# Layer 1's keys and queries by seven block products of a pair of row tiles, in place of row tile by row tile

## The chip, the cores and the metric

The kernel runs on one core of a Trainium2 chip. The metric is the device time of one execution in microseconds; less is better. Before the change it is 1144.76 us, the median of three runs (1144.38 to 1146.51).

## The reference, cut to what matters

Two layers, each a linear attention block and a gated MLP on x of 2048 rows by 512 columns, with residuals. Both layers use the same weights.

```python
def _A_ref(x, wqkv, wo):                 # H = 32 heads of 16 columns
    q, k, v = split(x @ wqkv)            # 512 -> 3 x 512
    phi = lambda t: jnp.where(t > 0, t + 1, jnp.exp(t)) + 1e-6
    pq, pk = phi(q), phi(k)
    kv = jnp.einsum("bhsd,bhse->bhde", pk, v)
    z = jnp.einsum("bhsd->bhd", pk)
    num = jnp.einsum("bhqd,bhde->bhqe", pq, kv)
    den = jnp.einsum("bhqd,bhd->bhq", pq, z)[..., None] + 1e-6
    return (num / den) @ wo
def _B_ref(x, w1, w3, w2):               # 512 -> 1792 -> 512
    return (silu(x @ w1) * (x @ w3)) @ w2
x = x + _A_ref(_layernorm(x), wqkv, wo);  x = x + _B_ref(_layernorm(x), w1, w3, w2)
x = x + _A_ref(_layernorm(x), wqkv, wo);  x = x + _B_ref(_layernorm(x), w1, w3, w2)
```

## The kernel before, in words

**Numbers in two parts.** Every operand of TensorE is a sum of two float16 numbers, a high and a low part. `mm` multiplies in three passes (high by high, low by high, high by low), so one product of 128 contracted rows is three matmuls.

**One layer.** `attention` goes over the 16 row tiles of 128 rows. For a tile, ACT normalises the row (`keys_rows`, `normalise`), its parts are made, and one DMA transpose of 8 blocks of 128 x 128 turns both parts (`keys_turn`); the turned rows are kept in HBM (`xt_d`) for the queries. The key product of a tile is 4 blocks of 128 features x 3 passes = 12 matmuls of 512 columns into one PSUM bank (`pk`). ACT reads the bank twice (L1257, L1258), takes an exponential, DVE joins them (L1268), and the result is split into parts again (L1316, L1325). `gram` multiplies the parts of keys by the parts of the rows, 12 matmuls of 512 columns a tile, into four banks (`gt0` to `gt3`) that add up over all rows. Then the Gram is scaled and split (L1362 to L1366), multiplied by the value weights (`kv`), masked, and multiplied by the output weights (`pm`), which gives a matrix `m_s`. The queries follow tile by tile: 12 matmuls (`pq`), phi, weighing (`weigh_in`, `weigh_out`), a transpose, 12 matmuls by `m_s` (`po`), and an add into the rows (`attn_add`). Layer 1's queries load their turned rows again from `xt_d`.

**The MLP** goes over passes of 512 rows and groups of hidden columns. It already uses a scheme of seven block products in place of eight (`P1` to `P7` in `mlp_group`): the rows are taken as quarters of two pairs of row tiles by two halves of features, the weights as quarters too, and sums of quarters are multiplied. Each of its products is of 256 columns; three of the seven banks' sums share a bank (`ba`, `bb`, `bc`), from which ACT copies and DVE adds between products. In layer 0's MLP a generator `background` prepares weights in the gaps (`HOOKS` says how many steps it takes after each group).

**The order.** The instructions of each engine stand in an order that is written out by hand: `ORDER` numbers the instructions of each engine as they were recorded and lists the numbers in the order in which they shall run; `arrange` adds that as dependences. An engine runs its list from first to last, so an instruction that waits holds all behind it.

## Time and profile before

| | |
|---|---|
| median of three runs | 1144.76 us |
| profiled execution | 1145.35 us, of which 1143.3 us span |
| granted clock of TensorE | 1.000 |
| busy share of the span | PE 99%, weight loads 75%, DVE 71%, ACT 56%, POOL 35% |
| DMA | 146.91 MB, mean 128 GB/s |
| layer 1's keys | from about 571 to 664 us |
| layer 1's queries | from about 664 to 753 us |

The span is the time from the first to the last instruction on the chip; the execution has about 2 us around it. PE is TensorE's matmuls and PEld its weight loads, DVE is VectorE, ACT is ScalarE, POOL is GpSimd, SP issues all the DMAs here. Nearly all matmuls stand on line 904, in `mm`, so the profile's rows are told apart by the bank that they write.

### The profile page before, as it was taken

How to read it: one execution, taken by the hardware profiler on the slowest of the kernel's cores; microseconds unless marked ns; L12 is line 12 of the kernel's file. 1: busy time of each engine (PE TensorE's matmuls, PEld its weight loads, DVE VectorE, ACT ScalarE, POOL GpSimd, SP SyncE). 2: the span in 40 equal slices, each digit the busy share in tenths (PEclk: the TensorE clock that was granted, in tenths of full speed). 3: DMA queues.
4: the chain of work that ended last, by engine and by line, in shares of the span. 5: the costliest groups of instructions: out<-in, count | busy, mean ns of one | idle time of the engine just before them, and what ended most of it. 6: DMA issues, size and time to landing. Idle time of an engine off the chain costs nothing.

```text
span 1143.3 us, 21778 instructions
## 1 busy us (share of the span) xinstructions
PE 1132.4 (99%) x8820; PEld 859.4 (75%) x8820; DVE 816.8 (71%) x1422; ACT 635.7 (56%) x1081; POOL 395.7 (35%) x494
## 2 busy tenths in 40 slices
PE   8999999999999999999999999999999999999998
PEld 3445445888888888888854454478888888888887
DVE  6888888897888888778773376748856566556556
ACT  6677878765545444334466644676544344353442
POOL 6641697411100304113674215761152120213113
PEclk9999999999999999999999999999999999999999
DMA  9996865796572221111343515955052350202001
GB/s 274 299 262 226 234 128 103 216 264 189 188 255 102 84 84 65 65 66 66 84 120 96 171 44 111 181 142 138 11 146 77 125 235 1 84 20 93 15 20 56
DMA packets 162549, 146.91 MB, mean 128 GB/s; under 512 B 129552, under 2 KB 138000, under 8 KB 157840
## 3 DMA queue, kind: packets, MB, share of 16 engines
q1 hardware_dynamic: 162448, 145.52, 43.5%
q8 instruction: 69, 1.13, 0.4%
q14 instruction: 32, 0.26, 0.1%
HBM read 72.35 MB, written 41.68 MB: 100 GB/s over the span
## 4 chain that ended last, share of the span: by engine, by line
PE 95%; DMA 2%; DVE 2%; POOL 0%; SPq 0%; issue 0%; ACT 0%; DVEq 0%; ACTq 0%; POOLq 0%
PE bb L904 25%; PE po L1740 20%; PE bc L904 13%; PE pq L904 7%; PE gt L904 7%; PE po L904 7%; PE ba L904 6%; PE pk L904 6%; PE po L1760 3%; DMA arena<-in_A_x_dram 1%; DMA arena<-arena 0%; PE kv L904 0%; PE pm L904 0%; DVE arena L828 0%; DVE st L866 0%
## 5 line engine op out<-in xcount | busy, mean ns | idle before, releaser
L904 PEld LDWEIGHTS <-arena 128*128 128x128 f16 x6360 | 618.0, 98 | 243.0 <-issue 4.6
L904 PE MATMUL bb<-arena 128*128 128x256 f16 x2688 | 349.0, 273 | 0.0
L1740 PE MATMUL po<-arena 128*128 128x256 f16 x2058 | 289.3, 273 | 0.0
L1695 ACT ACTIVATE arena<-bb 128x512 f32<-128x512 f32 x196 | 115.8, 594 | 209.8 <-PE bb L904 163.9
L1740 PEld LDWEIGHTS <-arena 128*128 128x128 f16 x2058 | 201.0, 98 | 24.4 <-ACT arena L1654 0.2
L904 PE MATMUL bc<-arena 128*128 128x256 f16 x1344 | 180.6, 273 | 1.4 <-DVE arena L1596 1.4
L1698 DVE TENSOR_TENSOR arena<-arena,bc 128x512 f32<-128x512 f32 x112 | 76.6, 684 | 87.4 <-ACT arena L1695 50.4
L1789 DVE SCALAR_TENSOR_TENSOR arena<-po,scalars,arena 128x256 f32<-128x256 f32 (+1 forms) x180 | 101.5, 585 | 34.6 <-PE po L1740 19.0
L1650 ACT ACTIVATE arena<-arena,scalars 128x512 f32<-128x512 f32 (+1 forms) x112 | 74.5, 666 | 85.9 <-DVE arena L1698 74.0
L1656 DVE TENSOR_TENSOR arena<-arena 128x1280 f16<-128x1280 f32 (+1 forms) x90 | 104.7, 1170 | 23.4 <-ACT arena L1654 23.3
L1654 ACT ACTIVATE arena<-arena 128x512 f16<-128x512 f32 (+1 forms) x112 | 100.9, 904 | 34.2 <-DVE arena L1669 15.7
L1651 DVE SCALAR_TENSOR_TENSOR arena<-arena,scalars 128x512 f32<-128x512 f32 (+1 forms) x112 | 79.2, 709 | 48.0 <-ACT arena L1650 46.5
L904 PE MATMUL ba<-arena 128*128 128x256 f16 x672 | 92.6, 273 | 0.0
L904 PE MATMUL pk<-arena 128*128 128x512 f16 x384 | 88.1, 379 | 2.9 <-DMA arena<-arena 1.8
L1656 POOL TENSOR_TENSOR arena<-arena 128x512 f16<-128x512 f32 x22 | 27.7, 1261 | 176.1 <-ACT arena L1654 133.1
L904 PE MATMUL gt<-arena 128*128 128x512 f16 x384 | 87.1, 379 | 0.2 <-POOL arena L1284 0.2
L904 PE MATMUL po<-arena 128*128 128x512 f16 x384 | 86.5, 379 | 0.0
L904 PE MATMUL pq<-arena 128*128 128x512 f16 x384 | 86.5, 379 | 0.0
L1797 POOL TENSOR_TENSOR arena<-arena 128x512 f32<-128x512 f32 x27 | 37.2, 1378 | 115.1 <-DVE arena L1789 115.1
L881 ACT ACTIVATE arena<-arena,nb_all,rs_all 128x512 f32<-128x512 f32 x64 | 51.0, 805 | 8.5 <-POOL nb_all L878 6.5
L1666 POOL TENSOR_TENSOR arena<-arena 128x256 f32<-128x256 f32 x10 | 7.6, 765 | 131.2 <-DVE arena L1651 131.2
L1581 POOL TENSOR_TENSOR arena<-arena 128x512 f16<-128x512 f32 x32 | 38.0, 1188 | 33.6 <-ACT arena L816 32.8
(163 smaller groups left out, 1279.6 us busy)
## 6 DMA issues: line engine op xcount, KB each, us to landing
arena<-xb_d SPq DMA_DIRECT2D x12, 1792.0 KB, 7.8
xb_d<-arena SPq DMA_DIRECT2D x8, 1792.0 KB, 7.3
xt_d<-arena SPq DMA_DIRECT2D x32, 256.0 KB, 2.6
arena<-xt_d SPq DMA_DIRECT2D x32, 256.0 KB, 3.2
arena<-in_B_w_dram SPq DMA_DIRECT2D x8, 896.0 KB, 5.8
arena<-in_B_w_dram SPq DMA_DIRECT2D x28, 256.0 KB, 3.6
w_d<-arena SPq DMA_DIRECT2D x4, 1792.0 KB, 8.1
arena<-w_d SPq DMA_DIRECT2D x4, 1792.0 KB, 8.2
```

The source lines that it names most:

```text
L881: nc.scalar.activation(dst, x_sb[:, t, :], AF.Identity, scale=rs_all[:, t : t + 1], bias=nb_all[:, t : t + 1],)
L904: nc.tensor.matmul(dst, lhs(a, k), rhs(b, k), start=first and k == 0 and i == 0, stop=last and k == n - 1 and i == len(PASSES) - 1, skip_g ...
L1581: low.tensor_tensor(nat[:, 1, :], to, nat[:, 0, :], OP.subtract)
L1650: nc.scalar.activation(t, gate, AF.Silu, scale=info["u1"])
L1651: nc.vector.scalar_tensor_tensor(t, up, info["hid"], t, OP.mult, OP.mult)
L1654: nc.scalar.activation(hs[:, 0, lo:hi], t[:, lo:hi], AF.Copy)
L1656: engine.tensor_tensor(hs[:, 1, lo:hi], t[:, lo:hi], hs[:, 0, lo:hi], OP.subtract)
L1695: nc.scalar.activation(dst, bank_, AF.Copy)
L1698: nc.vector.tensor_tensor(dst, dst, bank_, OP.add)
L1740: nc.tensor.matmul(po[:, i * HALF : (i + 1) * HALF], hs[:, a, qx, cs], w2[:, b, qw, :], start=g == ends[0] and i + a + b == 0, stop=g == e ...
L1789: nc.vector.scalar_tensor_tensor(dst, src, cb, to, OP.mult, OP.add)
L1797: engine.tensor_tensor(x0, x0, u[:, 0::2], OP.add)
```

## The change

In layer 1, `attention7` takes the place of `attention`. It goes over eight pairs of row tiles. A pair of tiles by two halves of features gives four quarters; four sums of quarters are made (DVE, L1573 to L1576), and all seven are turned by two DMA transposes, one of 12 blocks (the quarters that the Gram needs too) and one of 16 (the four sums). The weights of keys and queries are prepared in the same way in layer 0's last MLP passes (`att7`: seven parts of two halves each), the queries' stored in HBM (`q7_d`) and loaded in layer 1. A pair is then multiplied by `products7`: seven products of 6 matmuls of 256 columns, where three banks `kb`, `ka`, `kc` (`qb`, `qa`, `qc` for queries) take their sums, ACT takes out four of the results and DVE adds three. Later steps on keys and queries work on a pair at once (1024 columns). The Gram, the output product and the MLPs have the same matmuls as before.

```diff
+    def att7(name, i):
+        raw = view(AT_RAW, F32, NK, D)
+        nc.sync.dma_start(raw, wqkv_r[:, i])
+        ...
+        def part(n, src):
+            split_late(wk7[:, 0, :, n, :], wk7[:, 1, :, n, :], src, scale)
+        a11, a21, a12, a22 = quads
+        for n, src in ((0, a11), (1, a12), (2, a22)):
+            part(n, src)
+        for to, a, b, op in ((a22, a21, a22, OP.add), (a21, a11, a21, OP.subtract),
+                             (a11, a22, a11, OP.subtract), (a12, a12, a11, OP.subtract)):
+            nc.gpsimd.tensor_tensor(to, a, b, op)
+        for n, src in enumerate(quads):
+            part(3 + n, src)
...
+    def pair_turn(p, xts, nats):
+        b11, b21, b12, b22 = (q7[:, i, :] for i in range(4))
+        t = view(rows_at[1], F32, 4, HALF)
+        nc.vector.tensor_tensor(t[:, 0, :], b12, b11, OP.subtract)
+        nc.vector.tensor_tensor(t[:, 1, :], b22, t[:, 0, :], OP.subtract)
+        nc.vector.tensor_tensor(t[:, 2, :], b22, b12, OP.subtract)
+        nc.vector.tensor_tensor(t[:, 3, :], b21, t[:, 1, :], OP.subtract)
+        ...
+        xt = xts[p] = xt7_ring.next(F16, 28, P)          # two slots
+        nc.scalar.activation(hi0, q7[:, 0:2, :], AF.Copy)
+        nc.gpsimd.tensor_copy(hi1, q7[:, 2:4, :])
+        nc.gpsimd.tensor_tensor(lo0, q7[:, 0:2, :], hi0, OP.subtract)
+        nc.gpsimd.tensor_tensor(lo1, q7[:, 2:4, :], hi1, OP.subtract)
+        nc.sync.dma_start_transpose(xt[:, :12, :], nb[:, D:])
+        nc.scalar.activation(nt[:, 0], t, AF.Copy)
+        nc.gpsimd.tensor_tensor(nt[:, 1], t, nt[:, 0], OP.subtract)
+        nc.sync.dma_start_transpose(xt[:, 12:, :], nt.rearrange("p a q n -> p (a q n)"))
+        nc.sync.dma_start(xt7_d[:, p], xt)
...
+        product(bb, P1, True, False)          # 2 blocks of features x 3 passes, 256 columns
+        take(0, 0, bb)                        # ACT
+        product(bc, P5, True, False)
+        take(1, 1, bc)
+        product(bb, P6, False, False)
+        take(1, 0, bb)
+        product(bc, P3, False, True)
+        add(1, 0, bc)                         # DVE
+        product(bb, P7, False, False)
+        add(1, 1, bb)
+        product(ba, P2, True, True)
+        add(0, 0, ba)
+        between()
+        product(bb, P4, False, True)
+        take(0, 1, bb)
...
+        def query7(p):
+            ...
+            products7(xqs.pop(p), wq7, banks, *taken(r, info["u7q"], ones[:, 0:1]))
+            nc.scalar.activation(e, r, AF.Exp, bias=minus_one)
+            nc.vector.scalar_tensor_tensor(r, e, 1.0, r, OP.min, OP.max)
+            if p + 2 < NP:
+                load7(p + 2)                  # 896 KB
+        def weigh_out7(p):
+            ...
+                engine = nc.vector if p in (0, 2, 4, 6) else nc.gpsimd
...
-        attention(layer, ready, prep, before_gram)
+        (attention7 if layer else attention)(layer, ready, prep, before_gram)
...
 ORDER = {
     "PE": (
-        "0-56 69-80 57-68 93-104 84-89 117-128 81-83 90-92 105-107 111-116 141-152 108-110 "
...
```

`ORDER` is written anew for all engines and the whole program. `HOOKS` gives `background` 28 more steps after four groups in layer 0 (`0:0` becomes `7:0`), and group 3 of the MLP weights is fetched again at the start of layer 1's MLP, because its slot holds the new key weights.

The following rows show what stands in a row on an engine before and after, for the three places of which the prediction speaks. Repeated rows, and TensorE's weight loads, are left out.

TensorE, the middle of layer 1's keys, before: `pk` with its number is one tile's bank, each row 12 matmuls; `gt0` to `gt3` are the Gram's banks, each row 3 or 6 matmuls.

```order
L904 MATMUL pk_7194<-arena_66 128x512
L904 MATMUL pk_7240<-arena_66 128x512
L904 MATMUL gt2_6835<-arena_66 128x512
L904 MATMUL pk_7286<-arena_66 128x512
L904 MATMUL gt1_6834<-arena_66 128x512
L904 MATMUL gt0_6833<-arena_66 128x512
L904 MATMUL gt3_6836<-arena_66 128x512
```

The same place after, one pair from P1 to P4: P1 is the first row, then 3 matmuls each into two Gram banks, then P6, P5, P2, P7, P3 of 6 matmuls each, 3 Gram matmuls, P4, and the Gram's others.

```order
L945 MATMUL kb_7245<-arena_66 128x256
L945 MATMUL gt0_6954<-arena_66 128x512
L945 MATMUL gt1_6955<-arena_66 128x512
L945 MATMUL kb_7245<-arena_66 128x256
L945 MATMUL kc_7247<-arena_66 128x256
L945 MATMUL ka_7246<-arena_66 128x256
L945 MATMUL kb_7245<-arena_66 128x256
L945 MATMUL kc_7247<-arena_66 128x256
L945 MATMUL gt3_6957<-arena_66 128x512
L945 MATMUL kb_7245<-arena_66 128x256
L945 MATMUL gt2_6956<-arena_66 128x512
```

The tile by tile products have become narrow ones that come back to the same bank `kb` four times and to `kc` twice, with Gram matmuls between them.

ACT, the same stage, before: L1257 and L1258 read the bank, L1259 is the exponential, L816 a row's high part, L1316 a key's high part.

```order
L1257 ACTIVATE arena_66<-pk_7055,scalars_81 128x512
L1259 ACTIVATE arena_66<-arena_66 128x512
L1257 ACTIVATE arena_66<-pk_7102,scalars_81 128x512
L1258 ACTIVATE arena_66<-pk_7102,scalars_81 128x512
L1259 ACTIVATE arena_66<-arena_66 128x512
L816 ACTIVATE arena_66<-arena_66 128x512
L1258 ACTIVATE arena_66<-pk_7055,scalars_81 128x512
L1316 ACTIVATE arena_66<-arena_66,scalars_81 128x512 x2
```

After, for the pair whose products are shown above: L1632 takes a result out of a bank (here of P1, P6, P5 and P4, in this order), L1678 is the high part of the pair before, L1589 that of the four row sums of a later pair, L922 normalises, L1673 and L1674 are the Relu and the exponential.

```order
L1632 ACTIVATE arena_66<-kb_7245,scalars_81 128x256
L1678 ACTIVATE arena_66<-arena_66,scalars_81 128x1024
L1632 ACTIVATE arena_66<-kb_7245,scalars_81 128x256
L1589 ACTIVATE arena_66<-arena_66 128x1024
L1632 ACTIVATE arena_66<-kc_7247,scalars_81 128x256
L922 ACTIVATE arena_66<-arena_66,nb_all_91,rs_all_90 128x512 x2
L1632 ACTIVATE arena_66<-kb_7245,scalars_81 128x256
L1673 ACTIVATE arena_66<-arena_66,scalars_81 128x1024
L1674 ACTIVATE arena_66<-arena_66 128x1024
```

Between two takes that TensorE's next product needs there now stands an instruction of 1024 columns.

DVE, between the keys and the queries of layer 1, before: L1362 scales a Gram bank, L1366 makes a low part, L1270 to L1569 are the first steps on query tile 0.

```order
L1362 TENSOR_TENSOR arena_66<-gt1_6834,arena_66 128x512
L1362 TENSOR_TENSOR arena_66<-gt3_6836,arena_66 128x512
L1366 TENSOR_TENSOR arena_66<-arena_66 128x512 x2
L1362 TENSOR_TENSOR arena_66<-gt2_6835,arena_66 128x512
L1362 TENSOR_TENSOR arena_66<-gt0_6833,arena_66 128x512
L1366 TENSOR_TENSOR arena_66<-arena_66 128x512
L1270 SCALAR_TENSOR_TENSOR arena_66<-arena_66 128x512
L1552 SCALAR_TENSOR_TENSOR arena_66<-arena_66 128x512
```

After: L1716, L1730, L1733, L1747, L1748 and L1751 are the steps on query pair 0 (the first two, one and two instructions, stand ahead of the rows shown); L1776 scales a Gram bank, L1778 makes a low part, L1636 adds a product of query pair 1.

```order
L1733 TENSOR_REDUCE arena_66<-arena_66 128x32
L1747 TENSOR_SCALAR arena_66<-arena_66 128x32
L1776 TENSOR_TENSOR arena_66<-gt0_6954,arena_66 128x512
L1776 TENSOR_TENSOR arena_66<-gt2_6956,arena_66 128x512
L1748 RECIPROCAL arena_66<-arena_66 128x32 x2
L1751 TENSOR_TENSOR arena_66<-arena_66 128x512
L1776 TENSOR_TENSOR arena_66<-gt1_6955,arena_66 128x512
L1778 TENSOR_TENSOR arena_66<-arena_66 128x512
L1636 SCALAR_TENSOR_TENSOR arena_66<-qb_7720,scalars_81,arena_66 128x256
L1636 SCALAR_TENSOR_TENSOR arena_66<-qc_7722,scalars_81,arena_66 128x256
L1776 TENSOR_TENSOR arena_66<-gt3_6957,arena_66 128x512
L1778 TENSOR_TENSOR arena_66<-arena_66 128x512 x2
```

Steps on the queries, which stood behind the Gram's four banks, now stand ahead of and between them.

300 lines of the change are left out of this document (278 added, 22 removed), and 763 rows, old and new, of the table ORDER.

## The prediction

> **What bounds the kernel now.** I read the page first: which engine is never idle, at what clock, and which engine the chain that ended last runs through.
>
> ```profile
> PE 1132.4 (99%) x8820; PEld 859.4 (75%) x8820; DVE 816.8 (71%) x1422; ACT 635.7 (56%) x1081; POOL 395.7 (35%) x494
> PEclk9999999999999999999999999999999999999999
> PE 95%; DMA 2%; DVE 2%; POOL 0%; SPq 0%; issue 0%; ACT 0%; DVEq 0%; ACTq 0%; POOLq 0%
> ```
>
> A busy share of 99% does not prove much by itself, since the ends of matmuls are modelled. So I asked next what TensorE waited for over the whole run (its three longest rows: total us, times, longest) and what its timeline looks like in the stage that changes, layer 1's keys.
>
> ```profile
> PE pk L904 <- DMA arena<-arena: 1.8, 3, 0.8
> PE pm_k L765 <- DVE scalars L762: 1.6, 1, 1.6
> PE bc L904 <- DVE arena L1596: 1.4, 1, 1.4
> ```
>
> ```profile
> 605.41 2.75 PE L904 MATMUL pk<-arena 128*128 128x512 f16 x12
> 608.00 2.75 PE L904 MATMUL gt<-arena 128*128 128x512 f16 x12
> 610.59 5.34 PE L904 MATMUL pk<-arena 128*128 128x512 f16 x24
> 615.77 2.75 PE L904 MATMUL gt<-arena 128*128 128x512 f16 x12
> ```
>
> The reader should see the starts: 605.41, 608.00, 610.59, 615.77 are 2.59, 2.59 and 5.18 us apart, so 12 matmuls always take 2.59 us and no gap lies between key and Gram matmuls. The waits are single events of under 2 us. TensorE's queue is the kernel, and a matmul taken out of it is time taken out, as long as no other engine becomes late.
>
> The second question is what a matmul costs at the two widths. These are rows of the chain of waits, in order of time, the first from layer 1's keys, the second from the MLP, which already multiplies by seven block products of 256 columns:
>
> ```profile
> 648.96 5.18 PE pk L904 x24
> 766.13 3.93 PE bb L904 x36
> ```
>
> A 512-column matmul takes 5.18/24 = 0.2158 us, a 256-column one 3.93/36 = 0.1092 us. Half the width costs half the time (51%), although each has its own weight load.
>
> **What comes out of TensorE's queue.** Before, two row tiles of keys are 2 x 12 matmuls of 512 columns: 24 x 0.2158 = 5.18 us. After, a pair is 7 products x 2 blocks of 128 features x 3 passes = 42 matmuls of 256 columns: 42 x 0.1092 = 4.59 us. That is 0.594 us less for each pair; 8 pairs, keys and queries, make 16 x 0.594 = **9.5 us** less. Gram, output and MLP matmuls keep number and width. Nothing hides this gain and nothing is needed to release it: the queue has no gaps there. The most it can give is 1145.35 - 9.5 = 1135.85 for the profiled execution.
>
> The Trainium skill speaks against this: "TensorE: Matmul & The Clock Gate", section "Back-to-back issue gap", gives a stream of weight loads and matmuls about 81 ns a matmul at 128 columns and 131 ns at 512, so that halving the width saves much less than half. By it a pair would be an estimated 3.1 us before and 3.4 to 5.5 us after, a loss. This trace disagrees: 109 ns and 216 ns.
>
> **What the change adds beside TensorE.** The stages by windows (us; PE, PEld, DVE, ACT and POOL busy): two windows that hold about the last four of layer 0's twelve MLP passes, then layer 1's keys, then its queries. The five columns before the clock are the engines' busy time.
>
> ```profile
> 457.00:515.00 58.00, 58.00 (x534) 51.99 (x532) 43.02 (x72) 22.53 (x37) 10.30 (x9) 1.00 0.17 65
> 515.00:571.00 56.00, 56.00 (x515) 50.06 (x514) 44.11 (x82) 26.03 (x43) 25.54 (x29) 1.00 0.25 76
> 571.00:664.00 93.00, 93.00 (x476) 46.52 (x474) 45.23 (x74) 57.90 (x91) 42.58 (x83) 1.00 0.43 119
> 664.00:753.00 89.00, 89.00 (x463) 43.15 (x461) 65.37 (x132) 55.42 (x114) 48.39 (x54) 1.00 0.57 122
> ```
>
> The prices come from groups of instructions by shape (busy us, mean ns of one):
>
> ```profile
> L1257 ACT ACTIVATE arena<-pk,scalars 128x512 f32<-128x512 f32 x32 | 21.7, 681 | 36.9 <-PE pk L904 36.8
> L1258 ACT ACTIVATE arena<-pk,scalars 128x512 f32<-128x512 f32 x32 | 24.4, 767 | 0.0
> L1791 ACT ACTIVATE arena<-po,scalars 128x256 f32<-128x256 f32 x36 | 16.9, 469 | 30.4 <-PE po L1740 23.2 <-DVE arena L1797 4.6 <-POOL arena L1667 2.5
> L1631 ACT ACTIVATE arena<-arena 128x1024 f16<-128x1024 f32 x16 | 16.8, 1048 | 5.9 <-DVE arena L1627 3.8 <-POOL arena L1627 2.1
> L1789 DVE SCALAR_TENSOR_TENSOR arena<-po,scalars,arena 128x256 f32<-128x256 f32 x108 | 50.0, 478 | 17.3 <-ACT arena L1791 8.4 <-POOL arena L1798 6.0 <-PE po L1740 2.0
> L1667 DVE TENSOR_TENSOR arena<-arena 128x256 f32<-128x256 f32 x39 | 18.8, 482 | 0.3
> L1637 POOL TENSOR_TENSOR arena<-arena 128x1024 f16<-128x1024 f32 x9 | 19.8, 2205 | 2.1 <-ACT arena L1631 2.1
> ```
>
> *Keys, 93.0 - 4.75 = 88.2 us to do it in.* DVE: each pair gains three adds from PSUM (L1789's kind, 0.478) and four row sums (L1667's kind, 0.482), 3.36 us; 45.2 + 8 x 3.36 = 72.1 us, 82%. ACT: two passes over PSUM for each tile, 16 x (0.681 + 0.767) = 23.2 us, become four copies of a quarter and one pass of 1024 for each pair, 8 x (4 x 0.469 + 1.05) = 23.4 us; the high part of the four row sums adds 8 x 1.05 = 8.4; 57.9 + 8.6 = 66.5 us, 75%. POOL: the low part of the sums adds 8 x 2.2 = 17.6 to 42.6: 60.2 us, 68%. All fit, none by so much that order in the queue would be indifferent.
>
> *Order in ACT's queue.* What can hold TensorE is the shared bank: the next product into `kb` waits until ACT has copied the last one out, and P3 waits for the copy of P5 out of `kc`. From the end of P1 of a middle pair, P3 is due after two Gram groups (6 x 0.2158 = 1.29) and P6, P5, P2, P7 (4 x 0.655): 3.91 us. On ACT the copy after P6 starts at 1.95, then stands a 1024 pass (1.05) ahead of P5's copy: 1.95 + 0.47 + 1.05 + 0.47 = 3.94 and the hand-over. So P3 comes on time or about 0.2 us late, 0 to 1.4 us over the six pairs that look like this. Two rows of ACT's timeline say which end is nearer:
>
> ```profile
> 667.43 0.67 ACT L1261 ACTIVATE arena<-pq,scalars 128x512 f32<-128x512 f32 x1
> 668.00 0.68 ACT L1262 ACTIVATE arena<-pq,scalars 128x512 f32<-128x512 f32 x1
> ```
>
> Instructions of 0.68 us start 0.57 us apart, so sums of durations are upper bounds. I take 0.5 us.
>
> *Between keys and queries.* `kv` waits for all of the Gram's scaled parts. In the new order TensorE has 24 wide and 72 narrow matmuls between the last product of query pair 0 and `kv`: 24 x 0.2158 + 72 x 0.1092 = 13.0 us. DVE meanwhile must do the weighing of pair 0 and the Gram's parts, which the old order put mostly after:
>
> ```profile
> L1362 DVE TENSOR_TENSOR arena<-gt,arena 128x512 f32<-128x512 f32 x8 | 5.1, 682 | 0.1
> L1570 DVE RECIPROCAL den<-den 128x32 f32<-128x32 f32 x32 | 11.1, 348 | 2.3 <-ACT den L1556 1.9
> L1569 DVE TENSOR_SCALAR den<-den 128x32 f32<-128x32 f32 x20 | 7.8, 388 | 0.3
> L828 DVE SCALAR_TENSOR_TENSOR arena<-arena,scalars 128x1024 f16<-128x1024 f32 x8 | 10.1, 1277 | 0.0
> ```
>
> It starts after the product, its copy and the exponential, 0.66 + 0.47 + 1.05 = 2.2 us; then one of 1.28, thirteen of about 0.68, two each of 0.35 and 0.39 and two adds of 0.48: 12.5, so 14.7 against 13.0. That is up to 1.7 us late, and about 0.7 with starts 0.08 us closer than durations; I take 0.8. `pm` then has 18 narrow matmuls (1.97 us) as cover for a DVE, an ACT and a DVE step of some 0.65 each: 0 to 0.6 late, I take 0.3.
>
> *Queries, 89.0 - 4.75 = 84.3 us.* DVE gains 24 adds of 0.478, 11.5 us, and of its ten row normalisations, the two rows below, it keeps eight: 65.4 + 11.5 - 1.4 = 75.5 us, 90%. This is the tightest place.
>
> ```profile
> L1573 DVE TENSOR_TENSOR arena<-pq,den 128x512 f32<-128x512 f32 x7 | 4.8, 687 | 0.2
> L1573 DVE TENSOR_TENSOR arena<-arena,den 128x512 f32<-128x512 f32 x3 | 2.1, 685 | 0.0
> ```
>
> TensorE's order there puts output matmuls between P7 and P4, so I take 0.4 us, with 0 and 1.9 (half an add, 0.24, for each of eight pairs) as bounds.
>
> *Transposes and stores.* A pair is turned by one transfer of 12 and one of 16 blocks instead of two of 8, and stored and loaded in 896 KB instead of 2 x 256 KB. The nearest rows are the MLP's transposes of 14 blocks and the weights' transfers of 896 KB (us to landing):
>
> ```profile
> DMA to landing us min/median/max: 3.9/4.1/6.3
> w_d<-arena SPq DMA_DIRECT2D x3, 896.0 KB, 9.6
> arena<-w_d SPq DMA_DIRECT2D x3, 896.0 KB, 6.4
> ```
>
> A slot of the two for turned rows is free after P4 of pair p and wanted by P1 of pair p + 2, 42 wide and 42 narrow matmuls later: 13.6 us. Both transposes one behind the other need 8.2; with a store ahead of them 6.4 + 8.2 = 14.6, but P5, the first to read the second transfer, begins 0.655 + 1.29 + 0.655 = 2.6 us after P1, so 16.2 us are there. I cost it at nothing; the cover is those 13.6 us, and the bound is 0 to 1 us for each of six pairs.
>
> *Layer 0's last passes* gain the seven parts of both weights: 14 high parts on ACT, 14 low parts on DVE, 8 sums on POOL.
>
> ```profile
> L826 ACT ACTIVATE arena<-arena,scalars 128x512 f16<-128x512 f32 x38 | 26.3, 713 | 1.9 <-PE bb L904 0.9 <-DVE scalars L778 0.6 <-DMA arena<-in_B_w_dram 0.3
> L828 DVE SCALAR_TENSOR_TENSOR arena<-arena,scalars 128x512 f16<-128x512 f32 x38 | 29.1, 783 | 0.9 <-ACT arena L826 0.9
> L954 POOL TENSOR_TENSOR arena<-arena 128x512 f32<-128x512 f32 x4 | 5.1, 1269 | 14.7 <-DMA arena<-in_B_w_dram 14.0 <-DVE arena L828 0.6
> ```
>
> That is 10.0 us of ACT, 11.0 of DVE, 10.2 of POOL in 114 us, where DVE stands at 87.1: 98.1 us, 86%, and TensorE has no wait. Nothing on the path; bound 0 to 5.5 if half of DVE's part came in front of MLP steps.
>
> **The sum.** 1145.35 - 9.5 + 0.5 + 0.8 + 0.3 + 0.4 = 1137.85 for an execution like the profiled one, which stands 0.6 above the median of the runs (1144.76). So 1137.3.
>
> **The rivals.** (a) *The order holds:* waits from none to all bounds at once, 1.4 + 1.7 + 0.6 + 1.9 = 5.6 us: 1135.3 to 1140.9. For it: TensorE's short list of waits, though the MLP shares its banks in the same way. Chance 0.70. (b) *Evictions eat most of it:* copies and adds come late by 0.35 to 0.55 us for each of 16 pairs, 5.6 to 8.8 us: 1140.9 to 1144.1. For it, DVE at 90% in the queries; 0.12, of which 0.05 within 0.2% of no change. (c) *DVE becomes the bound of the queries, slower:* the add after P7 stands behind the three 1024-wide steps of the pair before (3 x 1.28 = 3.8 us) and P4 behind it; with three products as cover (1.96) some 1.9 us remain, 8 x 1.9 = 15 us, less 9.5: 1150. It decides from 9.5/8 = 1.2 us a pair (1.5 to be measured as slower). Against it: the output matmuls placed there, 2.59 us a tile. 0.09. (d) *Turned rows late* by 1.2 us for six pairs, 7 us: 1142.3; 0.03, half of it no change. (e) *Weight loads do not hide under narrow matmuls*, so that the saving isn't there: 18 more loads a pair at 98 ns are 1.76 us, less 0.594, 16 times:
>
> ```profile
> L904 PEld LDWEIGHTS <-arena 128*128 128x128 f16 x6360 | 618.0, 98 | 243.0 <-issue 4.6
> ```
>
> +18.7 us, 1163; the MLP's 0.1092 us speaks against it, 0.02. By the section named above it would be this one. (f) *Layer 0's added work shows:* 5.5 us, 1142.8 at worst; 0.04, of which 0.015 no change.
>
> **The numbers.** The likeliest is (a), 1137.3. The range goes from 1134.4, 0.9 below (a)'s lower end (half of the 1.8 us that TensorE waits for the opening's transposes, whose order is new too), to 1142.5, which takes in (a), half of (b), and parts of (d) and (f): about 0.8. 0.2% is 2.3 us, about what a measurement here can tell from no change. Faster: 0.70 + 0.07 + 0.015 of (d) + 0.025 of (f) = 0.81; same: 0.05 + 0.015 + 0.015 = 0.08; slower 0.09 + 0.02 = 0.11.
>
> **What would show it.** Right: narrow key and query matmuls 0.109 us apart; keys and queries together about 7.5 us shorter; TensorE's waits for `kb`, `kc`, `qb` on ACT or DVE under 3 us in all; one visible wait ahead of `kv`. Wrong: TensorE waiting for DVE's adds in the queries by more than 1 us a pair, for a transpose ahead of P1 or P5, or new waits in layer 0.

## The result, and the profile after

The changed kernel takes 1146.41 us (median of 22 runs, 1144.44 to 1153.02), the kernel before 1144.53 in the same comparison (22 runs): 1.0018 times as long, with a 95% interval of 1.0009 to 1.0026. It is slower by about 0.2%, where 0.65% faster was forecast, and lies outside the range of 1134.4 to 1142.5 us.

The page of the changed kernel's profile: busy time, granted clock, and the shares of the chain that ended last.

```profile
PE 1126.6 (98%) x9108; PEld 887.6 (78%) x9108; DVE 853.8 (75%) x1468; ACT 656.7 (57%) x1099; POOL 422.4 (37%) x477
...
PEclk9999999999999999999999999999999999999999
...
PE 86%; DVE 5%; ACT 3%; POOL 2%; DMA 2%; issue 1%; SPq 0%; DVEq 0%; POOLq 0%; ACTq 0%
```

TensorE is busy 5.8 us less than before, at the same clock, but the chain leaves it: 86% where it was 95%. What it waited for, longest first (total us, times, longest):

```profile
PE bc L945 <- DVE arena L2053: 1.9, 1, 1.9
PE po L945 <- DMA arena<-arena: 1.9, 1, 1.9
PE qc L945 <- ACT arena L1632: 1.2, 1, 1.2
...
PE gt L945 <- POOL arena L1652: 1.0, 1, 1.0
...
PE kc L945 <- DMA arena<-arena: 0.8, 1, 0.8
PE po L2095 <- DVE arena L2144: 0.7, 1, 0.7
PE qb L945 <- DVE arena L1636: 0.6, 1, 0.6
...
PE qa L945 <- DVE arena L1818: 0.6, 1, 0.6
```

There is no one culprit: every row shown is a single event, and DVE, ACT, POOL and the transposes are all among the releasers. The windows again, layer 0's last passes, then the keys and the queries at their new places (the last one ends some microseconds before the queries' last output matmuls):

```profile
457.00:515.00 58.00, 57.33 (x526) 51.15 (x524) 49.01 (x80) 30.04 (x49) 21.52 (x17) 1.00 0.38 130
515.00:571.00 56.00, 56.00 (x515) 50.20 (x513) 49.38 (x92) 31.18 (x49) 28.95 (x32) 1.00 0.26 74
571.00:660.00 89.00, 86.84 (x634) 61.55 (x632) 58.86 (x106) 65.30 (x88) 56.21 (x66) 1.00 0.77 202
660.00:745.00 85.00, 80.21 (x554) 52.09 (x553) 71.50 (x115) 52.01 (x92) 41.42 (x31) 1.00 0.57 129
```

Before, TensorE was busy for the whole of all four windows. Now 2.2 us are missing in the keys and 4.8 in the queries, though no other engine is full: DVE stands at 71.5 of 85 us there (84%), POOL at 41.4.

To see where time went I split the distance from TensorE's first matmul to its last in two: what its matmuls take one behind the other (0.216 us for 512 columns, 0.109 for 256; for the few other shapes the median distance of their starts), and the *gaps*, by which two starts lie further apart than that. Before: 1129.0 + 9.2 us. After: 1119.5 + 19.9. The matmuls are shorter by 9.5 us, as worked out (their distances are 0.109 and 0.216 us in both traces), and the gaps are longer by 10.7. The table gives the gaps of every kernel by stage (us from the span's start), worked out in the same way from the starts in each trace.

| kernel | opening, to 60 | layer 0, 60 to 300 | 300 to 571 | keys, 571 to 660 | queries, 660 to 720 | tail, from 720 | all | time, us | ratio to before (interval) |
|---|---|---|---|---|---|---|---|---|---|
| before | 7.6 | 1.7 | 0.0 | 0.0 | -0.1 | -0.1 | 9.2 | 1144.53 | 1 |
| after | 6.4 | 3.6 | 0.8 | 3.4 | 3.8 | 2.0 | 19.9 | 1146.41 | 1.0018 (1.0009 to 1.0026) |
| e1 | 7.4 | 2.3 | 0.8 | 2.0 | 3.8 | 2.0 | 18.2 | 1144.81 | 0.9998 (0.9989 to 1.0007) |
| e2 | 9.4 | 2.5 | 0.8 | 3.4 | 2.8 | 0.2 | 19.0 | 1143.96 | 0.9989 (0.9980 to 0.9997) |
| e3 | 8.1 | 3.9 | 0.8 | 3.4 | 0.9 | 1.2 | 18.3 | 1142.16 | 0.9977 (0.9969 to 0.9986) |
| e4 | 7.8 | 4.6 | 1.7 | 3.4 | 3.5 | 2.0 | 23.0 | 1149.89 | 1.0045 (1.0032 to 1.0057) |
| e5 | 9.2 | 4.7 | 0.2 | 6.1 | 5.5 | 9.2 | 34.8 | 1159.28 | 1.0127 (1.0114 to 1.0140) |
| e6 | 7.9 | 2.4 | 0.8 | 2.8 | 3.8 | 2.0 | 19.6 | 1146.32 | 1.0013 (1.0004 to 1.0022) |
| e7 | 6.3 | 3.7 | 0.8 | 1.4 | 0.0 | -0.1 | 12.0 | 1138.27 | 0.9940 (0.9927 to 0.9953) |
| e8 | 5.9 | 2.4 | 0.2 | 3.6 | 4.0 | 3.9 | 20.0 | 1147.29 | 1.0027 (1.0016 to 1.0037) |
| e9 | 6.2 | 3.5 | 0.8 | 3.5 | 3.8 | 2.2 | 19.8 | 1146.12 | 1.0015 (1.0006 to 1.0024) |
| e10 | 7.4 | 2.7 | 0.2 | 3.1 | 3.6 | 4.5 | 21.5 | 1146.41 | 1.0015 (1.0006 to 1.0023) |
| e11 | 6.9 | 2.5 | 0.8 | 3.4 | 4.7 | 2.9 | 21.2 | 1147.91 | 1.0026 (1.0017 to 1.0035) |
| e12 | 5.8 | 3.4 | 0.8 | 2.9 | 4.4 | 2.9 | 20.3 | 1147.43 | 1.0019 (1.0011 to 1.0028) |
| e13 | 6.0 | 3.6 | 0.8 | 3.4 | 2.8 | 2.6 | 19.2 | 1146.25 | 1.0011 (1.0003 to 1.0020) |
| e14 | 6.8 | 3.6 | 0.8 | 2.0 | 3.8 | 2.0 | 18.9 | 1145.86 | 1.0007 (0.9998 to 1.0016) |
| e15 | 7.8 | 2.1 | 0.8 | 2.0 | 2.8 | 4.3 | 19.8 | 1146.34 | 1.0011 (1.0002 to 1.0021) |
| e16 | 9.3 | 1.8 | 0.8 | 2.7 | 3.5 | 2.0 | 20.0 | 1145.08 | 1.0000 (0.9991 to 1.0008) |
| e17 | 9.3 | 1.7 | 0.2 | 3.5 | 3.5 | 1.7 | 19.9 | 1145.16 | 1.0002 (0.9993 to 1.0012) |
| e18 | 7.0 | 1.7 | 0.2 | 3.7 | 3.5 | 1.6 | 17.6 | 1144.93 | 0.9996 (0.9987 to 1.0005) |

The gaps are those of one profiled execution, the time is a median. After the first 7 us of the traces, seven stretches of 3.4 us, in which the granted clock is 0.50 and matmuls start at twice the distance, are counted as gaps of 1.3 to 1.7 us each: one in the openings of e2, e5, e16 and e17, two more in e5 (703 and 744 us) and one in e15's tail (the last section has rows of one). The opening's gaps run from 5.8 to 9.4 us, without those stretches to 8.1, over kernels whose queues are the same there, so 1 to 2 us are read by stage, not in the sum.

### The profile page after: what moved, and what is told of

The parts are those of the page before. It is cut to its first block, busy times and chain, and to the rows that moved or that the text cites. A ratio compares the mean times of both kernels' runs of the same rounds, so it can differ in the third digit from the quotient of the medians.

```text
span 1144.7 us, 22435 instructions
## 1 busy us (share of the span) xinstructions
PE 1126.6 (98%) x9108; PEld 887.6 (78%) x9108; DVE 853.8 (75%) x1468; ACT 656.7 (57%) x1099; POOL 422.4 (37%) x477
## 3 DMA queue, kind: packets, MB, share of 16 engines
q8 instruction: 71, 1.16, 0.4%
## 4 chain that ended last, share of the span: by engine, by line
PE 86%; DVE 5%; ACT 3%; POOL 2%; DMA 2%; issue 1%; SPq 0%; DVEq 0%; POOLq 0%; ACTq 0%
PE bb L945 25%; PE po L2095 19%; PE bc L945 13%; PE ba L945 6%; PE gt L945 6%; PE po L945 4%; PE pk L945 3%; PE po L2115 3%; PE pq L945 3%; DMA arena<-arena 1%; PE kb L945 1%; PE qb L945 1%; DVE arena L869 1%; POOL arena L1590 1%; ACT arena L1632 1%
## 5 line engine op out<-in xcount | busy, mean ns | idle before, releaser
L945 PEld LDWEIGHTS <-arena 128*128 128x128 f16 x6648 | 645.9, 98 | 215.4 <-issue 10.4
L2095 PE MATMUL po<-arena 128*128 128x256 f16 x2058 | 292.9, 273 | 0.7 <-DVE arena L2144 0.7
L2095 PEld LDWEIGHTS <-arena 128*128 128x128 f16 x2058 | 201.3, 98 | 24.2 <-DVE arena L2144 1.0
L2144 DVE SCALAR_TENSOR_TENSOR arena<-po,scalars,arena 128x256 f32<-128x256 f32 (+1 forms) x180 | 101.6, 585 | 30.8 <-PE po L2095 24.8
L2005 ACT ACTIVATE arena<-arena,scalars 128x512 f32<-128x512 f32 x112 | 74.5, 666 | 84.6 <-DVE arena L2053 70.7
L2006 DVE SCALAR_TENSOR_TENSOR arena<-arena,scalars 128x512 f32<-128x512 f32 x112 | 77.8, 695 | 38.1 <-ACT arena L2005 37.8
L945 PE MATMUL gt<-arena 128*128 128x512 f16 x384 | 89.4, 379 | 1.0 <-POOL arena L1652 1.0
L2011 POOL TENSOR_TENSOR arena<-arena 128x512 f16<-128x512 f32 x22 | 28.2, 1280 | 125.8 <-ACT arena L2009 96.8
L2153 POOL TENSOR_TENSOR arena<-arena 128x512 f32<-128x512 f32 x27 | 37.8, 1402 | 94.5 <-DVE arena L2144 94.5
L2152 POOL TENSOR_TENSOR arena<-arena 128x512 f32<-128x512 f32 x27 | 36.8, 1362 | 65.0 <-DVE arena L2144 63.5
L869 DVE SCALAR_TENSOR_TENSOR arena<-arena,scalars 128x512 f16<-128x512 f32 (+2 forms) x74 | 59.8, 822 | 1.1 <-ACT arena L867 0.9
L922 ACT ACTIVATE arena<-arena,nb_all,rs_all 128x512 f32<-128x512 f32 x64 | 50.7, 805 | 14.2 <-POOL nb_all L919 8.9
L867 ACT ACTIVATE arena<-arena,scalars 128x512 f16<-128x512 f32 (+2 forms) x74 | 52.1, 717 | 4.2 <-DVE scalars L819 1.8
```

What stands on the lines that cost most here:

```text
L867: nc.scalar.activation(hi, src, AF.Copy, scale=scale)
L869: lambda: nc.vector.scalar_tensor_tensor(lo, src, scale, hi, OP.mult, OP.subtract)
L922: nc.scalar.activation(dst, x_sb[:, t, :], AF.Identity, scale=rs_all[:, t : t + 1], bias=nb_all[:, t : t + 1],)
L945: nc.tensor.matmul(dst, lhs(a, k), rhs(b, k), start=first and k == 0 and i == 0, stop=last and k == n - 1 and i == len(PASSES) - 1, skip_g ...
L2005: nc.scalar.activation(t, gate, AF.Silu, scale=info["u1"])
L2006: nc.vector.scalar_tensor_tensor(t, up, info["hid"], t, OP.mult, OP.mult)
```

## The experiments

Theory 1: the matmuls' gain is all there, and comes back as waits for engines that the change loads. Theory 2: DVE and POOL hold each other up. Theory 3: the waits are only places in the queues, which were set anew. Theory 4: transfers. Line numbers are the changed kernel's.

### Cutting work out: e1, e2, e3, e7

```diff
e1 -nc.gpsimd.tensor_tensor(nt[:, 1], t, nt[:, 0], OP.subtract)
   +nc.gpsimd.tensor_tensor(nt[:, 1, :, :64], t[:, :, :64], nt[:, 0, :, :64], OP.subtract)
e2 -nat[:, lo:hi, 1, :], row(r), nat[:, lo:hi, 0, :], OP.subtract
   +nat[:, lo:hi, 1, :64], row(r)[:, :, :64], nat[:, lo:hi, 0, :64], OP.subtract
e3 -nc.vector.scalar_tensor_tensor(r, e, 1.0, r, OP.min, OP.max)
   +r_, e_ = r[:, :, 0, :P], e[:, :, 0, :P]
   +nc.vector.scalar_tensor_tensor(r_, e_, 1.0, r_, OP.min, OP.max)
   -row(e), row(r), EPS, zb[:, None, :].to_broadcast([P, n, D]), ...
   +row(e)[:, :, :P], row(r)[:, :, :P], EPS, zb[:, None, :P].to_broadcast([P, n, P]), ...
e7 = e1 + e2 + e3
```

> Leaves out three quarters of the low parts of the row sums (L1590 on POOL writes 64 of 256 columns of each sum), 8 passes of 2.2 us become about 0.6 us. Theory 1 (the 9.5 us are gained on TensorE and come back as waits for engines that the change loads; in the keys it is POOL, whose passes hold its own queue, hold DVE's instructions beside them, and send the transpose of the sums late): TensorE's gaps between 595 and 640 us fall from 3.4 to under 1 us, the largest two (1.16 at 604 behind POOL's copy L1652, 1.00 at 638 behind the transpose) go, DVE's L1679 and POOL's L1587, which took up to 2.0 us, are back at 1.28 and 1.16 throughout; time about 1144.0. Theory 3 (only the places in the queues, set anew, make the waits): the small waits at 610 and 621 stay, and so does most of the 638 one; gaps 2.5 us or more, time 1145.5 to 1146.4. Theory 4 (the store, the reload and the weights' loads make turned rows late): the 638 wait stays at 1.0 us, time 1145.2.

> Leaves out seven eighths of the low parts of the queries (L1758 on POOL writes 64 of 512 columns), 8 tile pairs' passes of 2.1 us become about 0.5 us or less. Theory 2 (DVE and POOL stand in each other's way: while a long POOL pass runs, DVE's passes of 1.22 us take up to 2.58): DVE's L1716 and L1730, of which the slowest took 2.33 and 2.58 us, all take 1.22 us; TensorE's gaps between 684 and 716 us fall from 3.7 to under 2 us, and the 2.08 us at 742, whose chain holds one such pass of 2.15 us, fall by more than half; time 1143.5 to 1144.5. Rival, theory 1 in the form that DVE alone is too full (90% of the stage): DVE's durations and the gaps up to 716 stay within 0.5 us, only 742 goes; time about 1144.5 to 1145. Theory 3: all of them stay, 1146.4.

> Leaves out three quarters of two of DVE's passes over a query pair (L1716 and L1730 work on 128 of 512 columns of each row), 16 passes of 1.22 us and more become about 0.45 us: some 13 us less on DVE between 660 and 745 us. Theory 1 (DVE at 90% is what TensorE waits for in the queries): the gaps at 687, 691 and 699 go (2.0 us), and the 2.08 us at 742 shrink by the 1.5 us that its chain spends there; time 1143 to 1144. Theory 3 (places in the queues): the 1.7 us at 712 to 716 (ACT's copies behind the MLP's rows) and 742 stay; time 1144.4 or more.

> The three cuts of the keys' low sums (L1590), of the queries' low parts (L1758) and of DVE's L1716 and L1730 in one kernel. If TensorE's 9.5 us are there and the loads of POOL and DVE alone take them back (theories 1 and 2), the gaps between 571 and 745 us fall from 9.9 to under 3 us, and the time is some 7 us under the changed kernel's: about 1139.5, faster than the kernel before by 5 us. If places in the queues hold as much (theory 3), 4 to 5 us of gaps remain there: 1141 to 1142.

e1: 1.4 of the keys' 3.4 us go, the wait at 604 with them; 638 falls from 1.00 to 0.57, the small ones at 610 and 621 stay. About half of what theory 1 wanted, and L1679 and L1587 still take up to 2.19 and 2.02 us. e2: the tail's 2 us go and 1.0 us in the queries; DVE's L1730 is at 1.22 us again on whole pairs, but one L1716 still takes 2.33 us, behind POOL's L1751, and the wait at 691 stays. e3: 2.9 us go in the queries, the 712 wait with them, which I had given to ACT's order, and 0.8 in the tail. e7: no gap at all is left from 660 us on. The window of the queries in e3 (columns as above), and then in e7:

```profile
660.00:745.00 85.00, 83.25 (x576) 54.41 (x575) 59.26 (x116) 53.67 (x94) 41.30 (x33) 1.00 0.59 137
```

```profile
660.00:745.00 85.00, 85.00 (x596) 56.27 (x595) 58.95 (x118) 56.16 (x100) 31.92 (x38) 1.00 0.60 131
```

In e7 TensorE is busy for 85.00 of 85.00 us, in the very order of queues that leaves it 4.8 us idle when the work is whole. So the change does give what it promises on TensorE (1138.27 us against 1144.95 for the kernel before in that comparison, with the waits of layer 0 still in it), and it is the elementwise passes that take it back. That much is shown. What e7 does not show is that it is only the passes that the change adds: its cuts take out work that the kernel before does too, and leave DVE with 59.0 us in that window, less than the 65.4 it had in the queries before.

### Transfers: e6

```diff
-nc.sync.dma_start(xt7_d[:, p], xt)
+n = 2 if p else 28
+nc.sync.dma_start(xt7_d[:, p, :n], xt[:, :n])
-nc.sync.dma_start(xqs[p], xt7_d[:, p])
+n = 2 if p > 2 else 28
+nc.sync.dma_start(xqs[p][:, :n], xt7_d[:, 0, :n])
```

> Leaves out most of the traffic of turned rows through memory: pairs 1 to 7 store 2 of 28 blocks, and the loads of pairs 3 to 7 bring 2 of 28 (896 KB down to 64 KB each; all loads read pair 0's place). Theory 4 (transfers make turned rows late): the 1.0 us at 638, ahead of which the transpose of the sums took 5.95 us to land, goes, and the 742 wait, which ends with a transpose, shrinks; gaps 1 to 2 us fewer, time 1144.5 to 1145.5. Theories 1 and 3: those gaps stay as they are, time 1146.4 +- 0.5.

638 falls from 1.00 to 0.37 us, nothing else in layer 1 moves, and the time stays (1146.32 us). Theory 4 is worth 0.6 us at most: in the trace of e16, below, where every transfer is whole, there is no wait at 638 at all, so this wait also comes and goes with when the transfers start.

### Other places in the queues: e4, e16, e5, e8

```diff
e4, e16: the numbers of ORDER between 60 and 300 us (e4), 172 and 260 us (e16) in the order of before
e5 POOL -L1590 L915 L916 L918 L1652          +L1652 L1590 L915 L916 L918
   ACT  -L1589 L1632(kc) L1632(kb)           +L1632(kc) L1632(kb) L1589
   DVE  -L1730 L1733 L1747 L1748 L1818 L1818 +L1818 L1818 L1730 L1733 L1747 L1748
   PE   -po x24, five products, P4(pair 6)   +po x12, P4(pair 6), po x12, five products
   ... (and the others that the expectation names)
e8 = e5's moves of L1652, of the V weights, of L2144, and of ACT's copies at 712
```

> The same work as the changed kernel; from 60 to 300 us of layer 0 the instructions of all five queues stand in the order that they had in the kernel before. Theory 3 (the order was set anew also where the change adds nothing, and cost 1.9 us there): TensorE's gaps between 60 and 300 us fall from 4.0 to about 2.1 us, time 1144.5. Rival (those waits vary from execution to execution, or come from what the change adds elsewhere): no change, 1146.4 +- 0.5.

> The same work as the changed kernel; as e4, but only from 172 to 260 us do the queues have the order of the kernel before, so that no seam falls where e4 lost 3.2 us (62 to 66 us) and 0.9 us (310). The gaps between 60 and 300 us, 2.3 to 3.9 us in the runs of the changed order so far, are 1.7 us as in the kernel before; time 1145 to 1146. Rival: a seam costs as much again, 1146.4 or more.

> The same work as the changed kernel, with some twenty instructions at other places in their queues. Keys: ACT's pass L1589 behind the copies out of kc and kb that it stood ahead of, for one pair the sums' passes (L1589, L1590) and their transpose ahead of the rows' own, POOL's L1652 ahead of L1590, the load of the V weights behind the next transpose. Queries: DVE's two last L1818 ahead of pair 1's L1730, ACT's copies of pair 6 ahead of the MLP's rows. Tail: TensorE's P4 of pair 6 twelve matmuls ahead of where it stood, and its copy, exponential and L1716 earlier. Layer 0: two of DVE's L869 behind L2053, one L2144 ahead of L2023. Theory 3 (the waits are places in the queues): TensorE's gaps fall from 3.4 to about 1 us in the keys, from 3.7 to 1.5 at 684 to 716, from 2.1 to under 0.8 at 742, from 0.84 to 0 at 468; with layer 0 about 7 us in all, time 1139 to 1141. Theory 1 (load: POOL's and DVE's passes are too long for the time they have, and another instruction becomes the late one): under half of that comes back, time 1143 to 1146.

> The same work as the changed kernel; of the moves of e5 only those whose own wait closed there without another beside it: POOL's L1652 ahead of one L1590, the load of the V weights behind the next transpose, one L2144 ahead of L2023 in layer 0, and ACT's four copies of 712 to 716 ahead of the MLP's rows. If these waits are slack in the queues (theory 3 in part), TensorE's gaps fall by 0.6 (300 to 571 us), 1.5 to 2 (571 to 660) and 1.5 (684 to 720): time 1142.5 to 1143.5. If queues are so full that each move makes another wait (what e5 showed of its moves together), 1145 to 1148.

e4 has the 1.5 us at 188 that the kernel before has, and pays more at its two seams. e16 has no bad seam: gaps of 1.8 us in layer 0, as before the change, and a median of 1145.08. So the re-made order of layer 0, at a time when the change adds nothing, costs 1 to 1.5 us (1146.41 beside 1144.53 for before, and 1145.08 beside 1144.70); 0.7 us of this can be the wait at 638, which is missing in e16's trace.

e5 fell: most moves closed the wait they were made for (468, 604, 687, most of 742), and yet the gaps grew by 15 us, with single ones of 2.9 us at 700 and 3.5 at 741 that were not there: what was moved ahead made something else late. Some 4.6 of the 15 us are the three stretches at half the clock, two of them at those long waits. e8 kept only the moves without a visible victim: 468 closes (0.6 us), 604 becomes a wait of 1.2 us for a transpose, the 712 wait changes its owner from ACT to DVE (1.5 us), and 1.7 us appear at 725. Theory 3 holds for layer 0; in layer 1 none of the moves tried here gained anything.

### Shorter chains and other engines: e9, e10, e11, e12

```diff
e9  -return [(0, 1), (1, 2)] if p in (0, NP - 1) else [(0, 2)]
    +return [(0, 1), (1, 2)] if p in (0, NP - 2, NP - 1) else [(0, 2)]
e10 = e8 + e9
e11 -nc.gpsimd.tensor_tensor(nat[:, lo:hi, 1, :], ...)   +(nc.vector if p in (1, 2, 3, 4, 5) else nc.gpsimd).tensor_tensor(...)
e12 = e11, and -nc.gpsimd.tensor_tensor(nt[:, 1], ...)   +(nc.vector if p in (3, 4, 5, 6, 7) else nc.gpsimd).tensor_tensor(...)
```

The wait at 742 in the changed kernel, in the chain that ended last, up to the output matmul of pair 6's first tile. The chain comes to pair 6 by an add of pair 7 that stands ahead of L1716 on DVE; pair 6's exponential on ACT ends at the same moment (731.99):

```profile
731.53 0.48 DVE arena L1636
...
732.02 1.24 DVE arena L1716
...
733.28 1.24 DVE arena L1730
...
734.54 1.23 DVE arena L1733
...
736.61 1.24 DVE arena L1751
...
737.87 1.07 ACT arena L1757
...
739.00 2.15 POOL arena L1758
...
741.16 3.21 DMA arena<-arena
...
744.42 1.68 PE po L945 x7
```

From 732.02 to 744.42 nothing in it waits for anything but the step before, and each step but the transpose is one of a whole pair.

> The same work as the changed kernel, but pair 6 of the queries is weighed tile by tile, as pairs 0 and 7 are (its L1730, L1733, L1751, L1757 and L1758 in two halves of 512). The 2.09 us at 742, where TensorE waits for tile 12 at the end of a chain of seven steps of a whole pair (1.24 + 1.22 + 0.20 + 0.55 + 1.22 + 1.06 + 2.14 us and the transpose), is a price of working by pairs: tile 12 is ready some 3 us sooner, the gap falls to under 0.3, time 1144.4. Rival (the chain's start sets it, since P4 of pair 6 stands late in TensorE's queue; or the extra instructions make DVE late elsewhere): gap of 1 us or more, time 1145.5 or more.

> The moves of e8 and the halves of e9 in one kernel. If both hold, gaps fall from 19.9 to about 14 us and the time to about 1141, faster than the kernel before by 3 to 4 us; if only e9 holds, 1144.5.

> The same work as the changed kernel, but the low parts of query pairs 1 to 5 (L1758) are made by DVE and not by POOL: 5 passes of 2.1 us fewer on POOL, 5 of some 1.2 us more on DVE, each put where DVE stood idle or between two passes. Theory 1 in the form that DVE's busy time is the bound of the queries: 6 us more on the fullest engine, the gaps between 684 and 745 us grow from 5.9 to 8 us or more, time 1148 or more. Theory 2 (POOL's long passes are the harm: slow themselves, and DVE's passes stand while they run): DVE's L1716 and L1730 take 1.22 us throughout, the gaps fall to 3 to 5 us, time 1143.5 to 1145.5.

> As e11, and the low parts of the keys' row sums (L1590) for pairs 3 to 7 are made by DVE too: 5 more passes of 2.2 us off POOL, 5 of some 1.2 us on DVE, which is two thirds busy there. Theory 2: the gaps between 571 and 660 us fall from 3.4 to under 2 us as in e1, though nothing is left out; time 1.5 us below e11's, 1142 to 1144. Theory 1 for DVE, or queues that make another wait of each move (as in e8): gaps of 3 us or more there, time not below e11's.

e9: 742 falls from 2.08 to 1.43 us, and 0.84 appear at 749. e10, the moves of e8 and these halves together, has 21.5 us of gaps where 14 were hoped for, and its time is e9's. Tile 12's data is ready at 738.20, but its transpose stands in SP's queue behind one of the MLP's (POOL's row, then two of SP's queue; in this kernel the lines are 22 higher):

```profile
737.04 1.16 POOL L1780 TENSOR_TENSOR arena<-arena 128x512 f16<-128x512 f32 x1 [0.93 <-ACT arena L1779]
...
737.93 1.30 SPq L2009 DMA_TRANSPOSE arena<-arena  x1
739.34 3.42 SPq L1789 DMA_TRANSPOSE arena<-arena  x2
```

e11 took five passes of 2.1 us off POOL and put five of some 1.2 on DVE: the gaps of queries and tail grow from 5.8 to 7.6 us. POOL's slow passes alone are not the cause, and DVE has no room for them. In the keys, where DVE is two thirds busy, e12 gains 0.5 us, a third of what e1 gained; its time is not measurably below e11's.

### Only the work that is new on DVE: e13, e14, e15

```diff
e13, e14 -dst = r[:, i, h, :]
         -nc.vector.scalar_tensor_tensor(dst, src, u, dst, OP.mult, OP.add)
         +dst = r[:, i, h, :n]           # n = 32: in the queries alone (e13), in the keys alone (e14)
         +nc.vector.scalar_tensor_tensor(dst, src[:, :n], u, dst, OP.mult, OP.add)
e14      and the four row sums of pair_turn on [..., :32]
e15 = e13 + e14
```

> Leaves out most of the adds that the change brings to the queries (L1636 works on 32 of 256 columns in the queries alone): 24 adds of 0.478 us become about 0.2, some 6.5 us less on DVE. Theory 1 for DVE (DVE's added work in the queries is what TensorE waits for): the gaps between 684 and 745 us fall from 5.9 to 3 us or less, time 1143 to 1144. Rival (the price is in the weighing by pairs, a chain of seven long steps that the adds only stand beside): 691 goes, 712 and 742 stay, gaps of 4.5 us or more, time 1145 to 1146.

> Leaves out most of DVE's added work in the keys (L1636 on 32 of 256 columns in the keys alone, and the row sums L1573 to L1576 on 32 of 256): 24 + 24 to 32 instructions of 0.48 and 0.42 us become about 0.2, some 12 to 14 us less on DVE. If DVE is what the keys wait for, the gaps between 571 and 660 us fall from 3.4 to under 1.5 us. If it is POOL's queue and ACT's order (e1, where POOL's work was cut and 1.4 us went), they fall by 0.5 us or less, and 604 and 638 stay.

> The cuts of e13 and e14 in one kernel: nearly all of DVE's work that the change adds to layer 1's attention is gone, POOL's and the pairs' long steps are there. If the price of the change is DVE's added work, the gaps between 571 and 745 us fall from 9.3 to under 4 us, time 1141; if half of it is POOL's work and the long steps, 6 us or more stay, time 1143 or more.

The window of the queries in e13:

```profile
660.00:745.00 85.00, 80.50 (x555) 52.25 (x554) 66.26 (x114) 52.18 (x92) 41.51 (x32) 1.00 0.56 128
```

DVE does 5.2 us less than in the changed kernel and stands at 66.3, about where the kernel before had it (65.4), and yet queries and tail still have 5.4 us of gaps; the time does not move. e3 cut 12.2 us of DVE and closed 3.7. By DVE's busy time alone e13 should have closed 1.6. So it is not chiefly how much DVE does: the passes over whole pairs, which stand in front of everything behind them, weigh more than the short adds. That the two kinds of work, not the two amounts, make the difference is argued here; no run took the same time from both. e15, with the cuts of e13 and e14 together, keeps 9.1 us of gaps from 571 us on, 1.7 of them a stretch at half the clock: DVE's added work is not where most of the price lies.

In the keys e14 closes the same 1.4 us as e1, which cut POOL and left DVE alone, mostly of the same two waits (604 and 638). The last section says how both can be for 604.

### Mended: e17, e18

```diff
e17 = e16's order of layer 0 + e9's halves + L2144 ahead of L2023
    SP   -L1987 L1767(tile 12)            +L1767(tile 12) L1987
    POOL -L1758(tile 13) L1992 L1992      +L1992 L1992 L1758(tile 13)
e18 = e17, and (nc.vector if p in (4, 5, 6, 7) else nc.gpsimd).tensor_tensor(nt[:, 1], ...)
```

> The same work as the changed kernel, with what single waits have shown so far: layer 0's queues between 172 and 260 us as in e16, L2144 ahead of L2023 (closed 0.6 us at 468 in e8), pair 6 in halves as in e9, and the two instructions that kept e9's halves from helping: tile 12's transpose ahead of one of the MLP's (in e9 its data stood ready at 738.2 us and the transpose was issued at 739.3), and the MLP's first two low parts (L1992) ahead of tile 13's (in e9 the 0.84 us at 749). If the wait at 742 is the length of pair 6's chain, it falls from 2.1 to under 0.4 us and none appears at 749; gaps in all 16 us, time 1142 to 1143.5, faster than the kernel before. If each step closed makes another late, 1145 to 1146.

> As e17, and the low parts of the keys' row sums of pairs 4 to 7 made by DVE (as in e12, without the pair that made a new wait of 0.5 us there). Gaps between 571 and 660 us 0.5 to 1 us under e17's, time 0.5 to 1 us under e17's; or no difference.

With the two obstacles gone the wait at 742 is closed (0.1 us), so it was the length of pair 6's chain. But 0.8 us stand at 745 for the next tile, and 0.8 in three pieces behind it: most is given back. The gaps are 19.9 us in all, where 16 were expected (1.6 of them a stretch at half the clock in the opening), and e18's keys gain nothing over e17's (3.7 and 3.5). Both kernels are where the kernel before is, 1.0002 and 0.9996 with intervals that hold 1. None of the kernels that do the whole work is measurably faster than before.

## Why the prediction was wrong, by its own steps

**What comes out of TensorE's queue, -9.5:** right to the tenth, 1129.0 to 1119.5 us. The section of the Trainium skill that spoke against it ("TensorE: Matmul & The Clock Gate", "Back-to-back issue gap") is contradicted by the new kernel as well: twelve wide matmuls start 2.59 us before what follows them and six narrow ones 0.65, so half the width is still half the time (rival (e) is out).

**Order in ACT's queue, 0.5:** the waits for `kb` and `kc` are there: 0.16, 0.37, 0.25, 0.17 and 0.19 us, 1.1 in all, inside the bound of 1.4. But the mechanism holds for two of them only: 0.37 (at 610) and 0.25 (at 621) stand behind L1589. In the other three ACT starts the copy when the product ends, and TensorE waits because a single product, 0.65 us, covers the copy; the prediction did not price that. Of ACT's rows, the first two are at 621, the third at 628:

```profile
619.80 1.04 ACT L1589 ACTIVATE arena<-arena 128x1024 f16<-128x1024 f32 x1
620.75 0.56 ACT L1632 ACTIVATE arena<-kc,scalars 128x256 f32<-128x256 f32 x1
...
628.05 0.56 ACT L1632 ACTIVATE arena<-kb,scalars 128x256 f32<-128x256 f32 x1 [0.62 <-PE kb L945]
```

One size was off, the copy out of PSUM, priced by L1791 at 0.469 us:

```profile
L1758 POOL TENSOR_TENSOR arena<-arena 128x1024 f16<-128x1024 f32 x6 | 13.8, 2293 | 11.8 <-ACT arena L1757 11.8
...
L1632 ACT ACTIVATE arena<-kb,scalars 128x256 f32<-128x256 f32 x24 | 13.4, 561 | 14.2 <-PE kb L945 14.2
...
L1716 DVE SCALAR_TENSOR_TENSOR arena<-arena 128x1024 f32<-128x1024 f32 x8 | 11.4, 1421 | 2.4 <-ACT arena L1715 2.4
...
L1730 DVE SCALAR_TENSOR_TENSOR arena<-arena 128x1024 f32<-128x1024 f32 x6 | 8.7, 1450 | 0.3
```

The copy takes 0.561: L1791 has a scale from memory, L1632 a scale and a bias. (The other three rows are the wide passes of the next paragraphs: DVE's were priced at 1.28, by L828, and take 1.42 and 1.45 on average.) The Trainium skill ("ScalarE: Activation LUTs", "What ACT_TABLE_LOAD costs") gives some 93 ns for each operand of that kind, and 92 ns is what the two rows differ by.

**"All fit" in the keys:** POOL's 60.2 us of 88.2 fit on average (measured 56.2 of 89; DVE's 72.1 were even 58.9), but the step stopped at busy shares. The 1.16 us at 604 is a small copy on POOL, L1652, that stands behind other work and then beside a pass of DVE (last section); I had priced no wait for POOL.

**Transposes and stores, 0:** 1.0 us at 638, in the bound; with less traffic 0.6 of it goes (e6), with a shorter low part on POOL 0.4 (e1).

**Between keys and queries, 0.8 for `kv`, 0.3 for `pm`:** no wait ahead of `kv`; 0.74 us behind `pm`, at 687, where P2 wants the bank that L1818 has not yet read.

**Queries, 0.4, with 1.9 as bound:** this is the step that failed: 3.8 us with the one behind `pm`, and 2.0 in the tail. It saw the place ("DVE 90%, the tightest place"; measured 84%) and then priced half an add for each pair. What was missing are the 1024-wide passes: a copy or an add that comes ready while one of them runs waits for all of it, and the last pair's seven steps end on TensorE's path. Rival (c) had the 1024-wide steps, but as a loss in every pair; they cost it at a few places only. That DVE and POOL also lengthen each other's passes, which makes up most of the wait at 691 and more than half of the one at 712, was in no term.

**Layer 0's last passes, 0:** here the added work does show, if little. The 0.8 us at 468 are a wait for L2144, which stands behind L2023 on DVE; L2023 takes 1.39 us there and not 0.41, beside L1304 on POOL, which is one of the sums that the change adds for the weights (rival (f), at 0.8 us and not 5.5). Two rows of DVE's timeline and one of POOL's:

```profile
467.36 1.39 DVE L2023 TENSOR_TENSOR arena<-arena 128x256 f32<-128x256 f32 x1
468.68 0.74 DVE L2144 SCALAR_TENSOR_TENSOR arena<-po,scalars,arena 128x512 f32<-128x512 f32 x1
```

```profile
465.79 5.50 POOL L1304 TENSOR_TENSOR arena<-arena 128x512 f32<-128x512 f32 x4 [1.08 <-ACT arena L2050]
```

What was left out is that the order was made anew in all of layer 0: 1.9 us more of gaps at 60 to 300 us in this profile, 0.4 to 2.2 over the traces with that order.

So what comes back was put at 2.0 us and is 10.7 (11.9 without the opening, which happens to be 1.2 shorter); keys and queries were to be 7.5 us shorter and are 0.2 (9.5 less 9.3 of gaps). TensorE's part was right; the bounds on the other engines were too low, because most of them were taken from sums over a stage. By its size the outcome lies between (b), evictions that eat most of it (5.6 to 8.8 us), and (c); by its mechanism it is neither, since the waits are a few single ones and not a loss in each pair.

## What to carry to other kernels

On a kernel whose TensorE queue has no gaps, a saving on TensorE is worth what the other engines leave of it, and that is not read from their busy shares: with DVE at 84% and POOL at half, 5.8 us of waits came in queries and tail. Follow one work item to the last use of its result and ask of each queue what the longest instruction is that can stand in front; joining two tiles into one saves instructions, but doubles the time for which others wait and the length of the last chain. Where DVE and POOL work side by side, look also at which of their passes run together. And to see whether a gain is there at all, cut the suspected work in the unchanged order (e7): it told more than all the moved instructions.
